# Attention and two feed-forward layers on one core: the probabilities of the later queries turned by DMA

## The chip, the core and the metric

The kernel runs on one core of a Trainium2 chip. TensorE multiplies matrices (PE in the rows, its weight loads PEld), VectorE (DVE) and ScalarE (ACT) work element by element, SyncE (SP) issues all the transfers; GpSimd (POOL) does next to nothing here. Operands lie in SBUF, matmul results in the banks of PSUM. The metric is the device time of one execution in microseconds. The kernel before took 786.69 us (median of 3 runs, 785.3 to 787.19).

## What is computed

Causal attention by blocks of 64 over 4 batches and 8 heads, 576 positions, 64 values a head; then two feed-forward layers on the 2304 tokens. Cut to what matters:

```python
scores = q @ k.T / sqrt(64); scores[block_i < block_j] = -1e9       # blocks of 64
attn = exp(scores - max) / (sum + 1e-9);  x = attn @ v              # (2304, 512)
h = x @ w_in; x2 = (max(h, 0) + log1p(exp(-abs(h)))) @ w_out        # 512 -> 2048 -> 512
h = x2 @ u_in; s = h * softmax(h)                                   # 512 -> 1024
out = ((s - mean) / sqrt(var + 1e-6) * g) @ u_out                   # 1024 -> 512
```

## The kernel before

All large products are made from operands split in two parts of the fast 32-bit matmul format (a high part and the remainder), three matmuls each, so that little precision is lost. Probabilities times v and the transposes run in plain float32.

The work falls into four kinds of tasks. **UnitA** (16 of them, a batch and a pair of heads each) does attention for the queries 0 to 255. **UnitC** (16) does it for the queries 256 to 575, in three tiles of scores `i` = 0, 1, 2: 128 queries of both heads against 384 keys, 128 against 512, and the last 64 queries of both heads, stacked in 128 rows, against 576. **Pair** (72) takes two blocks of 128 of the 2048 hidden columns of the first layer for a chunk of 256 tokens: two blocks of twelve matmuls into `hp`, the softplus, and two blocks of twelve into `acc` (`gh` and `gl` are the parts of its result). **Tok** (18) does the second layer for 128 tokens: 24 matmuls into `h`, the normalisation, and 24 into `op`. **Piece** converts weights. The pairs of the chunks 4 to 8 need what the UnitC tasks deliver, four units to 256 or more tokens; the second layer needs the weights u1 and u2, whose conversion starts when the last unit has left its memory.

Inside a unit C tile `i` goes: scores by `mm_qk` into the two banks of `S`, `mask`, `max`, `scale` (the maximum by 1/8), `exp` into `eC`, `den0`, `den1`, `norm`, then `tr` (lines 470 to 476), which turns every 128 x 128 block of `eC` on TensorE into the bank `T`, and `copy`, which brings `T` into `ps` (the last 64 keys of tile 2 into `p4`). `pv` multiplies `ps` and `p4` by v into `O`, and `x_hi` and `x_lo` split `O` for the pairs. In `eC`, `ps` and `p4` there is one buffer each, so tile `i` of the next unit can't be exponentiated before this unit's has been turned, and no copy into `ps` can start before the PV before it is through.

The order of every engine's instructions is fixed when the program is built. `Plan` simulates the tasks with a duration for each and puts on every engine, whenever it is free, the ready task of the lowest rank. The rank is a task's place plus `RANK` of its group plus `OFF` of its kind; tasks that two engines can do go where they would end sooner. Engines then run their lists strictly in order and wait where an operand is late.

The token stage has the technique that the change brings to the units: `split_hi` and `split_lo` copy the upper and lower 16 bits of `e` apart, `tr` (line 962) turns both halves by a DMA on SP's queue, and `merge` (line 965) puts them together again:

```python
SP.dma_start_transpose(out=self.hlt.bitcast(U16)..., in_=self.hl.bitcast(U16))
DVE.tensor_copy(self.ct.bitcast(U16)..., self.hlt.bitcast(U16)...)   # 2048 16-bit values a row
```

## Time and profile before

| what | value |
|---|---|
| median of 3 runs | 786.69 us |
| profiled execution | 785.26 us, its span 783.5 us |
| TensorE | busy 759.4 us (97%) |
| VectorE | busy 595.2 us (76%) |
| ScalarE | busy 416.6 us (53%) |
| opening, until TensorE is full | 0 to about 60 us |
| units C, first scores to last PV | 188 to 486 us |
| first h, first op | 548.5, 611.2 us |

Busy time counts matmuls and computing instructions; matmuls are pipelined, so their durations overlap. A name such as `eC<-S,mC` is what an instruction writes and reads; a line such as L236 can be that of a helper that many tasks use (228 makes all matmuls, 234 and 236 are copies on ScalarE and VectorE). The clock is the share of full speed that was granted to TensorE.

### The profile page before, as it was taken

Reading aid. Unit: us, or ns where it says so; the run is one execution under the profiler, and the core shown is the slowest. Engines: PE = TensorE matmul, PEld = TensorE weight load, DVE = VectorE, ACT = ScalarE, POOL = GpSimd, SP = SyncE. Lnnn points to the kernel's source line nnn. Section 1 sums busy time; section 2 is a strip of 40 time slices with the busy share of each in tenths; the row PEclk is TensorE's granted clock in tenths of the full one; section 3 lists DMA queues with packets and bytes.
Section 4 is the critical chain, followed back from the end, with each engine's and each line's share of the span. In section 5 each row is a group of like instructions: output and inputs, shape, how many; then the busy total and the mean of one; then the engine's idle time right before and its main releaser. Section 6 shows DMA issues by size and latency. Waiting matters only on the chain.

```text
span 783.5 us, 14248 instructions
## 1 busy us (share of the span) xinstructions
PE 759.4 (97%) x5608; PEld 675.4 (86%) x5608; DVE 595.2 (76%) x1326; ACT 416.6 (53%) x860; POOL 0.7 (0%) x6
## 2 busy tenths in 40 slices
PE   6679999999999999999999999999999999999998
PEld 4469899989888888888888889999998888888887
DVE  6999999475666677667766773766599998799882
ACT  6667765665566556556555554454484433333321
POOL 0000000000000000000000000000000000000000
PEclk9899999999999999999999999999999999999999
DMA  6554552211121112112111200323434453443323
GB/s 215 189 180 162 172 177 66 82 43 43 44 78 59 43 44 69 43 44 70 43 44 43 83 5 29 108 81 103 141 108 95 95 119 88 102 108 88 66 76 82
DMA packets 68643, 69.08 MB, mean 88 GB/s; under 512 B 40288, under 2 KB 51808, under 8 KB 68576
## 3 DMA queue, kind: packets, MB, share of 16 engines
q1 hardware_dynamic: 68576, 68.17, 30.0%
q8 instruction: 44, 0.72, 0.4%
q14 instruction: 23, 0.19, 0.1%
HBM read 49.29 MB, written 9.44 MB: 75 GB/s over the span
## 4 chain that ended last, share of the span: by engine, by line
PE 86%; DVE 10%; issue 1%; DMA 1%; ACT 1%; SPq 0%
PE acc L228 21%; PE hp L228 21%; PE op L228 13%; PE h L228 12%; PE S L228 5%; PE O L228 5%; PE T L476 5%; PE R L228 2%; DVE a L304 2%; DVE w L318 2%; DVE a L308 1%; PE r L228 1%; DVE mA L568 1%; DVE eA L589 1%; DVE t L681 1%
## 5 line engine op out<-in xcount | busy, mean ns | idle before, releaser
L228 PE MATMUL hp<-xt,w 128*128 128x256 f32 x1728 | 218.5, 280 | 2.2 <-DVE t L681 1.4
L228 PEld LDWEIGHTS hp<-xt,w 128*128 128x128 f32 x1728 | 205.4, 188 | 6.0 <-issue 2.7
L228 PE MATMUL acc<-gh,w 128*128 128x256 f32 x768 | 150.2, 285 | 3.5 <-DVE gh L236 3.5
L228 PEld LDWEIGHTS acc<-gh,w 128*128 128x128 f32 x768 | 123.4, 191 | 4.5 <-DVE gh L236 3.9
L228 PE MATMUL acc<-gl,w 128*128 128x256 f32 x384 | 107.6, 280 | 0.9 <-DVE gl L689 0.9
L228 PE MATMUL h<-u,w 128*128 128x512 f32 x432 | 100.4, 389 | 0.0
L228 PE MATMUL op<-w,w2w 128*128 128x512 f32 (+1 forms) x456 | 100.3, 378 | 0.0
L228 PEld LDWEIGHTS op<-w,w2w 128*128 128x128 f32 x456 | 82.5, 188 | 16.0
L228 PEld LDWEIGHTS h<-u,w 128*128 128x128 f32 x432 | 80.9, 188 | 16.6
L456 ACT ACTIVATE eC<-S,mC 128x384 f32<-128x384 f32 (+2 forms) x80 | 51.9, 653 | 52.3 <-DVE mC L445 52.3
L228 PEld LDWEIGHTS acc<-gl,w 128*128 128x128 f32 x384 | 73.1, 190 | 1.1 <-DVE gl L689 1.1
L672 ACT ACTIVATE t<-hp 128x512 f32<-128x512 f32 x72 | 42.7, 593 | 38.0 <-PE hp L228 37.9
L681 DVE SCALAR_TENSOR_TENSOR t<-hp,t 128x512 f32<-128x512 f32 x72 | 48.8, 678 | 17.5 <-ACT t L678 17.2
L689 DVE TENSOR_TENSOR gl<-t,gh 128x512 fp32r<-128x512 f32 x72 | 49.6, 689 | 5.6 <-ACT gh L234 4.5
L228 PE MATMUL acc<-gh,w2w 128*128 128x256 f32 x256 | 49.8, 284 | 0.0
L234 ACT ACTIVATE hl<-e 128x1024 bf16<-128x1024 bf16 x17 | 17.9, 1056 | 59.1 <-DVE e L922 59.1
L678 ACT ACTIVATE t<-t 128x512 f32<-128x512 f32 x72 | 45.5, 631 | 2.0
L675 ACT ACTIVATE t<-t 128x512 f32<-128x512 f32 x72 | 45.6, 633 | 1.8
L441 DVE TENSOR_REDUCE mC<-S 128x2 f32<-128x768 f32 (+2 forms) x48 | 46.3, 964 | 0.1
L234 ACT ACTIVATE ps<-T 128x512 f32<-128x512 f32 (+1 forms) x55 | 30.5, 555 | 29.3 <-PE T L476 29.3
L476 PE MATMUL T<-ident,eC 128*128 128x128 f32 x288 | 46.1, 278 | 0.0
L228 PEld LDWEIGHTS acc<-gh,w2w 128*128 128x128 f32 x256 | 40.8, 189 | 0.2 <-issue 0.2
(159 smaller groups left out, 1136.3 us busy)
## 6 DMA issues: line engine op xcount, KB each, us to landing
raw<-in_w_dram SPq DMA_DIRECT2D x32, 512.0 KB, 3.8
qkC<-in_qk_dram SPq DMA_DIRECT2D x16, 480.0 KB, 3.5
raw_u<-in_u_dram SPq DMA_DIRECT2D x11, 512.0 KB, 3.5
v<-in_vP_dram SPq DMA_DIRECT2D x16, 320.0 KB, 2.9
x2s<-stg SPq DMA_DIRECT2D x18, 256.0 KB, 2.2
xr<-x2s SPq DMA_DIRECT2D x18, 256.0 KB, 3.2
qkA<-in_qkA_dram SPq DMA_DIRECT2D x16, 256.0 KB, 3.5
out_dram<-ob SPq DMA_DIRECT2D x15, 256.0 KB, 2.9
```

The source lines that it names most:

```text
L228: PE.matmul(out, lhsT, rhs, start=start, stop=stop, skip_group_check=True)
L234: ACT.activation(out, a, AF.Copy)
L304: DVE.scalar_tensor_tensor(out=self.a, in0=self.raw[:, :, 1], scalar=-0x80000000, in1=self.a, op0=ALU.bitwise_and, op1=ALU.bitwise_or)
L318: DVE.tensor_sub(self.lo, self.af, self.hi)
L441: DVE.tensor_reduce(out=self.m[:, 0:n], in_=self.scores(i), axis=AX.X if i < 2 else AX.XY, op=ALU.max, negate=True)
L456: ACT.activation(e, sc, AF.Exp, scale=0.125, bias=m[:, j:j + 1], accum_out=den[:, j:j + 1])
L476: PE.transpose(T[:, 128 * k:128 * k + 128], e[:, 128 * k:128 * k + 128], ident)
L672: ACT.activation(self.t, self.hp, AF.Abs)
L675: ACT.activation(self.t, self.t, AF.Exp, scale=-1.0)
L678: ACT.activation(self.t, self.t, AF.Ln, bias=1.0)
L681: DVE.scalar_tensor_tensor(out=self.t, in0=self.hp, scalar=0.0, in1=self.t, op0=ALU.max, op1=ALU.add)
L689: DVE.tensor_sub(self.gl, self.t, self.gh)
```

## The change

The transposes of the units C leave TensorE. `norm` may now run on ScalarE too. Two `split`s per tile copy the lower and the upper 16 bits of the probabilities apart into a new tile `hl`, on ScalarE or VectorE; one DMA turns all blocks of the tile back into `eC`; two `merge`s (one for each head) bring them into `ps`, with `merge4` for `p4`. Tile 2 is padded by 64 columns for this. The bank `T` becomes a third bank of `S`, and the tiles take two of the three in turn. The factor 1/8 moves from `scale` and `exp` to the rounding of the queries, which makes `qk_hi` and `qk_lo` two instructions each. v has one buffer in place of two. The tables `OFF` and `RANK` are new throughout, so the order of everything is. In the token stage either half may be copied by ScalarE, and two dependences were added.

```diff
--- before.py
+++ after.py
-    "Pair.a": -81.8, "Pair.abs": 864.6, "Pair.b": -32.5, "Pair.do_gh": 2361.6, "Pair.do_gl": -1004.4,
+    "Pair.a": 788.0, "Pair.abs": 20664.3, "Pair.b": 1798.0, "Pair.do_gh": 10919.3, "Pair.do_gl": -8219.4,
...
+BANKS = (slice(0, 2), slice(0, 3, 2), slice(1, 3))
...
-            self.t_v = add("SP", dma_ns(327680), -8, self.load_v, [opened, self.t_qk] + g(p2, "t_pv") + g(p1, "t_v"), DMA_LAT)
-            sfree, tfree = (p1.sfree, p1.tfree) if p1 else ([], [])
-            self.t_tr, cps = [[], [], []], []
+            self.t_v = add("SP", dma_ns(327680), -8, self.load_v, [opened, self.t_qk] + g(p1, "t_pv", "t_v"), DMA_LAT)
+            self.t_tr, self.t_mg, self.t_exp, cps = [None, None, None], [[], [], []], {}, []
             for i, w in enumerate(WC):
-                r, heads = 7.0 * i, (0, 1) if i < 2 else (0,)
-                self.t_mm = t = add("PE", (600, 760, 860)[i], r, partial(self.mm_qk, i), [self.t_ql] + sfree)
+                r, heads = 7.0 * i, ((0, 1), (1, 0), (0,))[i]
+                free = [u.t_exp[x] for u, x in ((p1, (1, 0)), (p1, (2, 0))) if u] if i == 0 else \
+                       [self.t_exp[0, 0]] + ([p1.t_exp[2, 0]] if p1 else []) if i == 1 else [self.t_exp[0, 1], self.t_exp[1, 1]]
+                self.t_mm = t = add("PE", (721, 893, 797)[i], r, partial(self.mm_qk, i), [self.t_ql] + free)
                 if i < 2:
                     t = add("DVE", 140, r, partial(self.mask, i), [t])
-                t = chain("DVE", r, ((dve_ns(w * len(heads)), partial(self.max, i)), (140, partial(self.scale, i))), [t])
-                sfree = []
+                t = add("DVE", dve_ns(w * len(heads)), r, partial(self.max, i), [t])
+                e = []
                 for j in heads:
-                    sfree.append(add("ACT", 250 + .833 * w, r, partial(self.exp, i, j), [t] + sfree + (p1.t_tr[i] if p1 else [])))
-                t = chain("DVE", r, ((140, partial(self.den0, i)), (140, partial(self.den1, i))), sfree)
-                for j in heads:
-                    n = add("DVE", 70 + .55 * w, r, partial(self.norm, i, j), [t])
-                    for part in ((0,) if i < 2 else (0, 1)):
-                        m = 3 + i if i < 2 else (4, 1)[part]
-                        x = add("PE", 60 + 110 * m, r + 5, partial(self.tr, i, j, part), [n] + tfree)
-                        self.t_tr[i].append(x)
-                        c = add({"ACT": 110 + 107 * m, "DVE": 90 + 133 * m}, None, r + 4, partial(self.copy, i, j, part), [x] + g(p1, "t_pv"))
-                        tfree = [c]
-                        cps.append(c)
-            self.sfree, self.tfree = sfree, tfree
+                    e.append(add("ACT", 250 + .833 * w, r, partial(self.exp, i, j), [t] + e + (p1.t_mg[i] if p1 else [])))
+                    self.t_exp[i, j] = e[-1]
+                t = chain("DVE", r, ((140, partial(self.den0, i)), (140, partial(self.den1, i))), e)
+                n = [add({"ACT": 100 + .833 * w, "DVE": 70 + .55 * w}, None, r, partial(self.norm, i, j), [t]) for j in heads]
+                cols, back = w * len(heads), [p1.t_tr[i]] if p1 else []
+                n = [add({"ACT": 100 + .833 * cols, "DVE": 75 + .52 * cols}, None, r, partial(self.split, i, k), n + back) for k in range(2)]
+                self.t_tr[i] = add("SP", 300 + 1.6 * cols, r, partial(self.tr, i), n, 2600.0)
+                for j in range(2):
+                    self.t_mg[i].append(add("DVE", 75 + .52 * cols, r + 4, partial(self.merge, i, j), [self.t_tr[i]] + g(p1, "t_pv")))
+                if i == 2:
+                    self.t_mg[i].append(add("DVE", 205, r + 4, self.merge4, [self.t_tr[i]] + g(p1, "t_pv")))
+                cps += self.t_mg[i]
...
-            copy(e, self.qk[0], self.qr)
+            q, k = slice(0, 384), slice(384, 960)
+            if e == "ACT":
+                ACT.activation(self.qk[0][:, q], self.qr[:, q], AF.Copy, scale=0.125)
+                ACT.activation(self.qk[0][:, k], self.qr[:, k], AF.Copy)
+            else:
+                DVE.tensor_scalar(self.qk[0][:, q], self.qr[:, q], 0.125, None, op0=ALU.mult)
+                DVE.tensor_copy(self.qk[0][:, k], self.qr[:, k])
 
         def qk_lo(self):
-            DVE.tensor_sub(self.qk[1], self.qr, self.qk[0])
+            q, k = slice(0, 384), slice(384, 960)
+            DVE.scalar_tensor_tensor(out=self.qk[1][:, q], in0=self.qr[:, q], scalar=0.125, in1=self.qk[0][:, q],
+                                     op0=ALU.mult, op1=ALU.subtract)
+            DVE.tensor_sub(self.qk[1][:, k], self.qr[:, k], self.qk[0][:, k])
...
-            self.v = self.t([128, 2, 5, D], "v")
+            self.v = self.t([128, 2, 5, D], "v", 1)
...
-            return state["S"][:, :, 0:WC[i] if i < 2 else WC[2] // 2]
+            return state["S"][:, BANKS[i], 0:WC[i] if i < 2 else WC[2] // 2]
...
-        def scale(self, i):
-            DVE.tensor_scalar(self.m[:, 0:self.n], self.m[:, 0:self.n], 0.125, None, op0=ALU.mult)
...
-            ACT.activation(e, sc, AF.Exp, scale=0.125, bias=m[:, j:j + 1], accum_out=den[:, j:j + 1])
+                e = e[:, 0:WC[2]].rearrange("p (a b) -> p a b", a=2)
+            ACT.activation(e, sc, AF.Exp, bias=m[:, j:j + 1], accum_out=den[:, j:j + 1])
...
-        def norm(self, i, j):
-            e = state["eC"][i][:, j, :]
-            DVE.tensor_scalar(e, e, self.stat[i][1][:, j:j + 1], None, op0=ALU.mult)
-
-        def tr(self, i, j, part):
-            T, e = state["T"], state["eC"][i][:, j, :]
-            if part:
-                PE.transpose(T[0:64, 0:128], e[:, 512:576], ident)
-                return
-            for k in range(3 + i if i < 2 else 4):
-                PE.transpose(T[:, 128 * k:128 * k + 128], e[:, 128 * k:128 * k + 128], ident)
-
-        def copy(self, i, j, part, e):
-            T, ps, p4 = state["T"], state["ps"], state["p4"]
-            if part:
-                copy(e, p4, T[0:64, 0:128])
-            elif i < 2:
-                copy(e, ps[:, 0:3 + i, j, 128 * i:128 * i + 128], T[:, 0:384 + 128 * i].rearrange("p (t q) -> p t q", q=128))
+        def norm(self, i, j, e):
+            p, r = state["eC"][i][:, j, 0:WC[i]], self.stat[i][1][:, j:j + 1]
+            if e == "ACT":
+                ACT.activation(p, p, AF.Copy, scale=r)
             else:
-                copy(e, ps[:, :, :, 256:320], T.rearrange("p (t j q) -> p t j q", t=4, j=2))
+                DVE.tensor_scalar(p, p, r, None, op0=ALU.mult)
+
+        def split(self, i, n, e):
+            p = state["eC"][i].rearrange("p j w -> p (j w)").bitcast(U16).rearrange("p (c two) -> p c two", two=2)
+            to = state["hl"][i].bitcast(U16).rearrange("p (two c) -> p two c", two=2)
+            cols = WC[i] * (2 if i < 2 else 1)
+            copy(e, to[:, n, 0:cols], p[:, 0:cols, n])
+
+        def turned(self, i):
+            return state["eC"][i].rearrange("p j w -> p (j w)").bitcast(U16)
+
+        def tr(self, i):
+            SP.dma_start_transpose(out=self.turned(i).rearrange("p (c q) -> p c q", q=128), in_=state["hl"][i].bitcast(U16))
+
+        def merge(self, i, j):
+            ps = state["ps"].bitcast(U16)
+            if i < 2:
+                src = self.turned(i).rearrange("p (two j t q) -> p j t q two", two=2, j=2, q=128)[:, j]
+                dst = ps[:, 0:3 + i, j, 256 * i:256 * i + 256]
+            else:
+                src = self.turned(i).rearrange("p (two t j q) -> p j t q two", two=2, j=2, q=64)[:, j, 0:4]
+                dst = ps[:, :, j, 512:640]
+            DVE.tensor_copy(dst.rearrange("p t (q two) -> p t q two", two=2), src)
+
+        def merge4(self):
+            src = self.turned(2).rearrange("p (two t q) -> p t q two", two=2, q=128)[0:64, 4]
+            DVE.tensor_copy(state["p4"].bitcast(U16).rearrange("p (q two) -> p q two", two=2), src)
...
-        state["S"] = q.tile([128, 2, 512], F32, name="S")
-        state["T"] = q.tile([128, 512], F32, name="T")
+        state["S"] = q.tile([128, 3, 512], F32, name="S")
         state["O"] = q.tile([128, 512], F32, name="O")
-        state["eC"] = [state["pat"].tile([128, 2 if i < 2 else 1, w], F32, name=f"eC{i}") for i, w in enumerate(WC)]
+        state["eC"] = [state["pat"].tile([128, 2 if i < 2 else 1, w], F32, name=f"eC{i}") for i, w in enumerate((WC[0], WC[1], WC[2] + 64))]
+        state["hl"] = [state["pat"].tile([128, (2 * w if i < 2 else w + 64)], F32, name=f"hl{i}") for i, w in enumerate(WC)]
+        DVE.memset(state["hl"][2], 0.0)
...
-            self.t_sp = [add({"ACT": 950, "DVE": 610}, None, rank, self.split_hi, [t_c, t_w] + o2("t_tr")),
-                         add("DVE", 610, rank, self.split_lo, [t_c, t_w] + o2("t_tr"))]
+            self.t_sp = [add({"ACT": 950, "DVE": 610}, None, rank, partial(self.split, i), [t_c, t_w] + o2("t_tr")) for i in range(2)]
             t_s = chain("DVE", rank, [(75, partial(self.small1, i)) for i in range(4)], [t_c])
             t_s = add("ACT", 335, rank, self.logexp, [t_s])
             self.t_s = chain("DVE", rank, [(75, partial(self.small2, i)) for i in range(3)], [t_s] + o3("t_ob"))
             self.t_tr = add("SP", 3000, rank + .5, self.tr, self.t_sp + o2("t_mg"), DMA_LAT)
             self.t_mg = add("DVE", 1140, rank, self.merge, [self.t_tr] + o2("t_ll"))
-            self.t_lh = add({"ACT": 950, "DVE": 610}, None, rank, self.ln_hi, [self.t_mg] + o2("t_b"))
-            self.t_ll = add("DVE", 1140, rank, self.ln_lo, [self.t_lh])
+            self.t_lh = add({"ACT": 950, "DVE": 610}, None, rank, self.ln_hi, [self.t_mg, pairs[-1].t_b1] + o2("t_b"))
+            self.t_ll = add("DVE", 1140, rank, self.ln_lo, [self.t_lh, pairs[-1].t_b1] + o2("t_b"))
...
-        def split_hi(self, e):
-            self.hl, self.hlt, self.ct = (state[x][self.t % 2] for x in ("hl", "hlt", "ct"))
-            kind = BF16 if e == "ACT" else U16
-            copy(e, self.hl.bitcast(kind)[:, DF2:], self.half(1, kind))
-
-        def split_lo(self):
-            self.hl, self.hlt, self.ct = (state[x][self.t % 2] for x in ("hl", "hlt", "ct"))
-            DVE.tensor_copy(self.hl.bitcast(U16)[:, 0:DF2], self.half(0, U16))
+        def split(self, i, e):
+            self.hl, self.hlt, self.ct = (state[x][self.t % 2] for x in ("hl2", "hlt", "ct"))
+            halves = self.e.bitcast(U16).rearrange("p (f two) -> p f two", two=2)
+            copy(e, self.hl.bitcast(U16)[:, DF2 * i:DF2 * i + DF2], halves[:, :, i])
```

Where an order stands below, a row is line, operation, what it writes and reads, the shape and a count. On TensorE in the units, where `T` is the bank of the transposes, `S` that of the scores, and `hp` and `acc` belong to pairs; before:

```order
L228 MATMUL hp_114<-xt,w_8_89 128x256 x12
L476 MATMUL T<-ident,eC_2173 128x128 x4
L228 MATMUL hp_114<-xt,w_9_90 128x256 x12
L228 MATMUL S<-qkh 128x512 x2
L228 MATMUL S<-qkl,qkh 128x512 x2
L228 MATMUL S<-qkh,qkl 128x512 x2
L473 MATMUL T<-ident,eC_2173 64x128
L228 MATMUL acc<-gh,w_4_101 128x256
```

and now:

```order
L230 MATMUL hp_114<-xt,w_8_89 128x256 x12
L230 MATMUL hp_114<-xt,w_9_90 128x256 x12
L230 MATMUL S<-qkh 128x512 x2
L230 MATMUL S<-qkl,qkh 128x512 x2
L230 MATMUL S<-qkh,qkl 128x512 x2
L230 MATMUL acc<-gh,w_4_101 128x256
```

The groups into `T` are gone from between the pair blocks and the scores; the rest of the piece stands as it did.

On VectorE from the maximum of a tile 2 to that of a later tile (`qkl` is the low part of the next unit's q and k, `t` and `gl` are a pair's); before:

```order
L441 TENSOR_REDUCE mC<-S 128x1
L413 TENSOR_TENSOR qkl<-qkC,qkh 128x960
L445 TENSOR_SCALAR mC<-mC 128x1
L236 COPY ps<-T 128x4x128
L460 TENSOR_SCALAR dC<-dC 128x1
L464 RECIPROCAL dC<-dC 128x1
L468 TENSOR_SCALAR eC_2173<-eC_2173,dC 128x576
L436 MEMSET S 64x2x64
L681 SCALAR_TENSOR_TENSOR t<-hp_115,t 128x512
L441 TENSOR_REDUCE mC<-S 128x2
```

and now:

```order
L453 TENSOR_REDUCE mC<-S 128x1
L238 COPY hl_2158<-eC_2155 128x1024
L423 SCALAR_TENSOR_TENSOR qkl<-qkC,qkh 128x384
L425 TENSOR_TENSOR qkl<-qkC,qkh 128x576
L501 COPY ps<-eC_2154 128x3x256 x2
L468 TENSOR_SCALAR dC<-dC 128x1
L709 TENSOR_TENSOR gl<-t,gh 128x512
L472 RECIPROCAL dC<-dC 128x1
L479 TENSOR_SCALAR eC_2156<-eC_2156,dC 128x576
L448 MEMSET S 64x2x64
L238 COPY hl_2159<-eC_2156 128x576
L453 TENSOR_REDUCE mC<-S 128x2
```

The scaling of the maximum and the copy out of `T` have gone; splits (`hl<-eC`) and merges (`ps<-eC`) of other tiles have come between, and a pair's `gl` now stands behind the merges of the next unit's tile 0.

## Rows read from the trace of the kernel before

**Rows 1.** Page, busy tenths of 40 equal slices of the span, by engine.

```profile
PE   6679999999999999999999999999999999999998
...
DVE  6999999475666677667766773766599998799882
```

**Rows 2.** Windows from PV to PV: length, busy us (instructions) by engine, clock, DMA.

```profile
317.62:336.00 18.38, 18.38 (x156) 16.25 (x157) 12.73 (x34) 10.46 (x21) 0.00 (x0) 1.00 0.17 47
336.00:354.27 18.27, 18.27 (x156) 16.14 (x157) 12.72 (x34) 10.45 (x21) 0.00 (x0) 1.00 0.16 46
...
sum 201.61, PE 201.61 PEld 178.16 DVE 140.27 ACT 116.89 POOL 0.00; mean PE 18.33 PEld 16.20 DVE 12.75 ACT 10.63 POOL 0.00
```

**Rows 3.** Chain that ended last, shares of the span by engine, tile, line.

```profile
by line: PE acc L228 21.5%; PE hp L228 21.3%; PE op L228 12.5%; PE h L228 12.5%; PE S L228 4.9%; PE O L228 4.8%; PE T L476 4.6%; PE R L228 1.9%; DVE a L304 1.8%; DVE w L318 1.5%; DVE a L308 1.4%; issue 1.3%; PE r L228 1.2%; DVE mA L568 1.1%
```

**Rows 4.** Timeline of TensorE, one unit: start us, us, instruction, count.

```profile
322.23 0.43 PE L228 MATMUL S<-qkh,qkl 128*128 128x288 f32 x2
...
331.52 0.60 PE L476 MATMUL T<-ident,eC 128*128 128x128 f32 x4
331.87 1.62 PE L228 MATMUL hp<-xt,w 128*128 128x256 f32 x12
```

**Rows 5.** The same chain in order of time, after the units: start, us, what.

```profile
509.23 2.72 PE acc L228 x24
```

**Rows 6.** Groups by line and shape, VectorE: count, busy us, mean ns, idle before.

```profile
L965 DVE COPY ct<-hlt 128x2048 uint16<-128x2048 uint16 x18 | 21.9, 1218 | 5.4 <-DMA hlt<-hl 5.4
...
L468 DVE TENSOR_SCALAR eC<-eC,dC 128x512 f32<-128x512 f32 x32 | 14.4, 480 | 0.2
...
L959 DVE COPY hl<-e 128x1024 uint16<-128x1024 uint16 x18 | 12.4, 692 | 0.4
...
L236 DVE COPY ps<-T 128x512 f32<-128x512 f32 x14 | 9.7, 692 | 10.1 <-PE T L476 10.1
...
L236 DVE COPY ps<-T 128x384 f32<-128x384 f32 x11 | 6.1, 552 | 0.2 <-PE T L476 0.2
...
L445 DVE TENSOR_SCALAR mC<-mC 128x2 f32<-128x2 f32 x32 | 5.1, 161 | 0.6
...
L236 DVE COPY p<-T 64x128 f32<-64x128 f32 x15 | 4.2, 283 | 0.0
...
L236 DVE CAST xt<-O 128x192 fp32r<-128x192 f32 x8 | 2.8, 354 | 6.6 <-PE O L228 6.6
```

**Rows 7.** The same groups, ScalarE.

```profile
L234 ACT ACTIVATE ps<-T 128x512 f32<-128x512 f32 x34 | 20.3, 597 | 19.6 <-PE T L476 19.6
...
L234 ACT ACTIVATE hl<-e 128x1024 bf16<-128x1024 bf16 x17 | 17.9, 1056 | 59.1 <-DVE e L922 59.1
...
L234 ACT ACTIVATE ps<-T 128x384 f32<-128x384 f32 x21 | 10.3, 488 | 9.8 <-PE T L476 9.8
```

**Rows 8.** DMA issues: count, KB each, median us from issue to landing.

```profile
qkC<-in_qk_dram SPq DMA_DIRECT2D x16, 480.0 KB, 3.5
v<-in_vP_dram SPq DMA_DIRECT2D x16, 320.0 KB, 2.9
...
hlt<-hl SPq DMA_TRANSPOSE x18, 4.3
```

**Rows 9.** Timeline of VectorE, the same unit: the normalisation of the last scores.

```profile
327.28 0.52 DVE L468 TENSOR_SCALAR eC<-eC,dC 128x576 f32<-128x576 f32 x1
```

**Rows 10.** Windows of 20 us, opening.

```profile
20.00:40.00 20.00, 12.00 (x84) 8.45 (x82) 19.08 (x52) 13.46 (x36) 0.00 (x0) 0.83 0.62 198
```

**Rows 11.** Timelines of VectorE and TensorE around the first h.

```profile
537.62 0.69 DVE L318 TENSOR_TENSOR u<-a_u,u 128x512 fp32r<-128x512 f32 x1
...
548.51 11.06 PE L228 MATMUL h<-u,w 128*128 128x512 f32 x48
```

**Rows 12.** Timeline of all engines at the end.

```profile
747.05 33.11 PE L228 MATMUL op<-w,w2w 128*128 128x512 f32 x168
...
771.87 1.23 DVE L975 TENSOR_TENSOR w2w<-ct,w2w 128x1024 fp32r<-128x1024 f32 x1
```

More of the change, by code (lines that the diff above doesn't have):

```diff
@@ L30 @@
-    "Piece.do_lo@P": 1123.5, "Piece.do_lo@P0": -1265.3, "Piece.do_lo_g": -389.9, "Piece.load": 727.8,
-    "Piece.load@P0": -81.6, "Tok.a": 281.7, "Tok.aggr": -1508.4, "Tok.bm": 1627.8, "Tok.center": -2327.7,
-    "Tok.exp": 1006.4, "Tok.ln_hi": 147.1, "Tok.ln_lo": 1789.8, "Tok.load": -1361.3, "Tok.logexp": -1108.4,
-    "Tok.max": -2583.3, "Tok.merge": 1445.4, "Tok.mul": 348.2, "Tok.o_evac": -1055.5, "Tok.small1": -386.7,
-    "Tok.small2": -428.2, "Tok.split_hi": 1311.4, "Tok.split_lo": -1105.9, "Tok.stats": 584.7, "Tok.store": -419.8,
@@ new lines @@
+    "Pair.evac": 675.0, "Pair.exp": -7474.3, "Pair.ln": -9835.0, "Pair.store": -5836.4, "Pair.stt": 7547.0,
+    "Piece.abs": 10964.5, "Piece.abs@P0": 2481.0, "Piece.bits0": 2651.5, "Piece.bits0@P0": -10740.6,
+    "Piece.bits1": -5638.9, "Piece.bits1@P0": 1504.7, "Piece.bits2": -6724.4, "Piece.bits2@P0": 8160.9,
+    "Piece.do_hi": 6783.4, "Piece.do_hi@P0": 8530.5, "Piece.do_hi_g": 2688.1, "Piece.do_lo": 4827.0,
+    "Piece.do_lo@P": -4177.2, "Piece.do_lo@P0": -15153.1, "Piece.do_lo_g": -860.1, "Piece.load": 10384.6,
@@ new lines @@
+    "Piece.load@P0": 11156.8, "Tok.a": -3408.6, "Tok.aggr": -9655.0, "Tok.bm": 2985.1, "Tok.center": -10058.0,
+    "Tok.exp": 13414.8, "Tok.ln_hi": 6845.7, "Tok.ln_lo": 3377.4, "Tok.load": -6979.6, "Tok.logexp": -4391.2,
+    "Tok.max": 7574.5, "Tok.merge": -6856.4, "Tok.mul": -2725.4, "Tok.o_evac": 6544.2, "Tok.small1": 5810.6,
+    "Tok.small2": -1482.8, "Tok.split": -6804.0, "Tok.split_hi": -9056.3, "Tok.split_lo": -9326.4,
+    "Tok.stats": -5464.0, "Tok.store": 22167.6, "Tok.tr": -13756.9, "Tok.x_hi": -11484.4, "Tok.x_lo": -1305.6,
[11 rows of a table added]
@@ L50 @@
+    "UnitC.copy": -4765.8, "UnitC.den0": 5224.6, "UnitC.den1": -6300.5, "UnitC.exp": -5258.0, "UnitC.load_qk": 3996.6,
+    "UnitC.load_v": -4166.3, "UnitC.mask": -654.7, "UnitC.max": -9211.3, "UnitC.merge": 1083.9,
+    "UnitC.merge4": 3115.7, "UnitC.mm_qk": -3221.1, "UnitC.norm": 5503.0, "UnitC.pv": -8282.1, "UnitC.qk_hi": 34.6,
+    "UnitC.qk_lo": -14155.2, "UnitC.split": -696.2, "UnitC.tr": -11789.9, "UnitC.x_hi": 13549.6,
+    "UnitC.x_lo": -4037.3, "UnitC.xx": 5329.0,
 }
 RANK = {
[3 rows of a table removed]
-    "Tok": (798.2, 267.06),
[3 rows of a table added]
@@ L56 @@
+    "Tok": (18449.2, 1582.9),
 }
@@ L429, in mm_qk @@
                         h = slice(64 * j, 64 * j + 64)
-                        mm(S[:, j, 0:w], q[h, 128 * i:128 * i + 128], k[h, 384:384 + w], n == 0, n == 2)
+                        mm(S[:, j], q[h, 128 * i:128 * i + 128], k[h, 384:384 + w], n == 0, n == 2)
                     else:
-                        mm(S[:, j, 0:w // 2], q[:, 256:384], k[:, 384 + w // 2 * j:384 + w // 2 * (j + 1)], n == 0, n == 2)
+                        mm(S[:, j], q[:, 256:384], k[:, 384 + w // 2 * j:384 + w // 2 * (j + 1)], n == 0, n == 2)
         def mask(self, i):
-            DVE.memset(state["S"][0:64, :, WC[i] - 64:WC[i]], MASKED)
+            DVE.memset(self.scores(i)[0:64, :, WC[i] - 64:WC[i]], MASKED / 8)
         def max(self, i):
@@ L441, in max @@
             DVE.tensor_reduce(out=self.m[:, 0:n], in_=self.scores(i), axis=AX.X if i < 2 else AX.XY, op=ALU.max, negate=True)
-            self.n = n
-        def scale(self, i):
-            DVE.tensor_scalar(self.m[:, 0:self.n], self.m[:, 0:self.n], 0.125, None, op0=ALU.mult)
             self.stat = getattr(self, "stat", {})
-            self.stat[i] = (self.m, self.den, self.n)
+            self.stat[i] = (self.m, self.den, n)
         def exp(self, i, j):
@@ L763, in open_3 @@
         p3 = left.enter_context(pool("p3", "left"))
-        for x in ("hl", "hlt", "ct"):
+        for x in ("hl2", "hlt", "ct"):
             state[x] = [p3.tile([128, DF2], F32, name=f"{x}{i}") for i in range(2)]
```

14 lines of the change are left out of this document (1 added, 13 removed), and 28 rows, old and new, of tables (OFF, RANK).

## The prediction

> **What bounds the kernel now.** I read the slices of the page first. TensorE's line is at nine tenths from the fourth slice to the end; only the opening (slices of 19.6 us at 6, 6 and 7 tenths) has gaps, together about 21 us, and there VectorE's line rises to nine [rows 1]. So from about 60 us on the end is set by how much TensorE has to do. Next the windows cut at the PV matmuls of the attention units (the 16 units of queries from 256 on): eleven periods are 18.33 us each on average, TensorE is busy for all of it, VectorE for 12.75 us, ScalarE for 10.63 [rows 2]. In this stage a microsecond taken from TensorE shortens the run, as long as the others can follow. The chain of waits agrees: it is on TensorE nearly throughout and gives the transposes into T 4.6% [rows 3]. The profiled execution took 785.26 us, 1.76 us more than its span of 783.5, and lies 1.4 us under the median of 786.69; my sum starts from 785.26.
>
> **TensorE.** Removed are 19 transposes in each unit, 304 in all; scores and PV matmuls stay as they are. What one is worth has three readings. From start to start a group of four holds the engine for 0.35 us [rows 4], 0.09 each, 27 us for 304: the lower end, since it counts nothing that is lost ahead of a group's first start. By the chain, 4.6% of 783.5 is 36.0 us, 2.25 in a unit [rows 3]. By difference: 24 pair matmuls in a row take 2.72 us [rows 5], so a unit's 96 take 10.9; with some 2.4 for scores (the chain's 4.9% for S over 16 units) and 2.35 for PV (its 4.8%), 18.33 leaves 2.7 us, or 43 us for 16 units [rows 2, 3]. I take the chain's 36.0, the middle one: it counts what the end was delayed by. TensorE then needs 18.33 - 2.25 = 16.1 us a unit.
>
> **VectorE.** The 16-bit copies are not new to this kernel: the token stage does the same even-and-odd copies. 1024 values take 0.692 us and 2048 take 1.218, so 0.167 us plus 0.513 ns a value [rows 6]. The new order puts 50 of the 96 splits on VectorE: 19 of 768 values (0.561), 15 of 1024 (0.692), 16 of 576 (0.463), 28.4 us. The merges are all on VectorE: 32 of 768, 32 of 1024, 32 of 512 (0.430) and 16 of 256 (0.298), 58.5 us. The subtraction for qkl becomes two instructions, 16 x 0.167 = 2.7, and six more 512-wide casts come over, 2.9. Gone are 48 scalings (0.161, 7.7 us), the copies out of T (9.7 + 6.1 + 4.2 = 20.0 us), 37 normalisations that go to ScalarE (at 0.480, 17.8) and 20 casts of the output (at 0.354, 7.1) [rows 6]. Net +40 us, 2.5 a unit: 12.75 + 2.5 = 15.3 of 16.1 us, 95%. Starts follow each other a little closer than these durations say, so 92% may be nearer. VectorE is not the bound by this sum, but it has hardly a microsecond left in a unit, which is the weak spot of the forecast.
>
> **ScalarE.** 1024 values take 1.056 us there and 512 take 0.597, so about 0.14 us plus 0.9 ns a value [rows 7]. It takes 46 splits (13 of 768, 17 of 1024, 16 of 576: 39 us), 37 normalisations (about 0.55: 20) and 20 output casts (about 0.3: 6), and loses the copies out of T (20.3 + 10.3) and six casts (3.6) [rows 7]: +31 us, 1.9 a unit, 12.6 of 16.1 us. Covered.
>
> **The transposes by DMA.** 48 are added, of 1536, 2048 and 1280 16-bit columns. The token stage has the widest one already: it lands 4.3 us after its issue [rows 8]. I take 4.3 for all three; the smaller ones can be quicker. They go through SP's queue between the loads of v and qk. v has one buffer now, so its load waits for the PV before; in the order it stands ahead of the second transpose, which is not ready until the scores that precede that PV have been turned into probabilities, so nothing ready stands behind it.
>
> On this the Trainium skill speaks against the change: "VectorE: DVE Perf Modes", section "The three transpose paths", gives 390 ns for a 128x128 block on TensorE and 1309 ns by DMA, and its rules say to use TensorE where PSUM will do. A unit moves 12 + 16 + 10 = 38 such 16-bit blocks; at that price an estimate is 49.7 us a unit, far beyond 16.1, and the sum would be a loss of hundreds of microseconds. The trace does not bear it out: sixteen blocks land together in 4.3 us.
>
> **Does the chain within a unit still fit?** Before, the last scores of a unit end at 322.66 and their normalised row is done at 327.80, 5.1 us later [rows 4, 9]. From there the new path is split 0.65, landing 4.3, merges 2 x 0.43 + 0.30, with hops between engines about 0.5: 6.6 us, 11.7 in all. On TensorE the new order leaves 11.2 to 15.1 us of other work between those scores and PV (seven to nine pair blocks of some 1.4 us and the next unit's scores); in six units it is 11.4. VectorE's own work in the same stretch, summed along the order, is 6.8 to 14.0 us and leaves 1.0 to 4.6. So some units may wait a few tenths, 0 to 6 us in all; I take 2.
>
> **Opening and token stage.** The order of the opening is nearly the old one; six casts of weights leave VectorE and a copy of 768 comes, under 2 us either way: 0. After the last PV the u1 pieces are converted one at a time, and their last subtraction starts at 537.62 while the first h starts at 548.51 [rows 11]: 10.2 us to spare. The order leaves 36 pair matmuls less in between, 4.1 us: still covered. At the end 120 output matmuls of full width stood between the last h and the last output block, 27 us; now 96, 21.8. The chain they cover ran from 747 to 773.1, 26 us, but with VectorE and ScalarE busy with the token before; its own steps come to some 17. Taken at 0; at worst 4 us [rows 12]. Sum: 785.26 - 36.0 + 2 = **751.3 us**.
>
> **Rivals.** *VectorE sets the pace of the units.* At 95% of the period, with every instruction in a fixed order, a late landing or a late exponential stops everything queued behind it, the pairs' subtractions too, and TensorE then waits for those. For it: VectorE waited 5.6 us of each 18.33 before, and 0.8 would be left. Against: much of that was waiting for TensorE, which itself comes sooner. One microsecond a unit gives 751.3 - 2 + 16 = 765; from 756 to 780. Such gaps should not cost the clock: its mean of 0.83, a mixture of the levels 1.2 and 2.4 GHz, stands where TensorE was busy 12 of 20 us [rows 10], and here it would be busy 16 of 17.
>
> *Slower: the 16-bit copies cost more than in the token stage.* Here the merges write runs of 256 values into strided rows of ps and the splits read two heads. If each such value cost 1.9 times the row's, the 5.4 us a unit would be 10.3 and VectorE 20.2 us a unit, against 18.33 now: 785 + 16 x 1.9 = 815. It decides from 1.6 times on, where VectorE reaches 18.33. Against: they pick every other 16-bit value just as L959 and L965 do, on one side of the copy.
>
> *Slower: the transposes go one behind the other, with the loads.* If no transpose overlapped another transfer, a unit would need 3 x 4.3 us, 3.5 for qk and 2.9 for v [rows 8], 19.3 us against 18.33: 785 + 16 = 801. It decides from 18.33 on. Against: in the token stage the landing stays at 4.3 although loads run beside it in the same queue. The block price of the Trainium skill ("VectorE: DVE Perf Modes", "The three transpose paths") would be the extreme of this rival and shares its chance.
>
> *The gain does not come.* The longer path through the DMA holds a unit at 18.3 us although TensorE has less to do; 785.
>
> *Better.* The new order also closes part of the opening's 21 us; 735 to 742.
>
> **How the numbers follow.** Forecast 0.66 (742 to 756: the three readings of the transposes and 0 to 6 us of waits); VectorE sets the pace 0.22; copies dearer 0.04; transposes in a row 0.03; no gain 0.02; better 0.03. The range 742 to 768 holds the forecast and about two thirds of the first rival, 0.8. About 0.3% is what a measurement of this kernel can tell from no change, 2.4 us. Faster 0.66 + 0.22 + 0.03 = 0.91, same 0.02, slower 0.07.
>
> **What would show it.** Right: periods between PVs near 16.1 us times the pair blocks in them, TensorE busy throughout, VectorE above 90% there; the transposes landing in 3 to 4.5 us; merges of 1024 near 0.69. Wrong: idle time of TensorE ahead of PV or of acc matmuls, released by the merges or by gl; VectorE at ten tenths over the units; landings over 6 us.

## The result, and the profile after

The changed kernel took 762.22 us (median, 761.21 to 762.49) where the kernel before took 786.94 beside it: 0.9686 of the time, 95% interval 0.9669 to 0.9704, 24.7 us less. The forecast was 751.3, 35.4 below the median of 786.69 known then. The time lies in the range of 742 to 768, above the 742 to 756 of the forecast's own case.

The profiled execution took 761.21 us, its span is 759.3 (before 783.5): 24.2 less. Its page, busy time and then the slices that answer [rows 1]:

```profile
PE 729.9 (96%) x5304; PEld 645.3 (85%) x5304; DVE 638.4 (84%) x1376; ACT 441.0 (58%) x907; POOL 0.7 (0%) x6
...
PE   6779999999999999999999999999999999999998
...
DVE  6999999576888998888898995767999988888882
```

TensorE's line is as full as it was, and VectorE's has risen to eight and nine tenths from the eleventh slice to the twenty-fourth, where the attention units lie. The windows that answer [rows 2], first from the first PV to the last, then the one unit with a full set of scores and eight blocks of pair matmuls, as nearly all periods of the kernel before have (length, busy us and count by engine, clock, DMA share, GB/s):

```profile
211.59:464.83 253.24, 251.22 (x2053) 219.76 (x2053) 225.28 (x500) 185.35 (x378) 0.00 (x0) 1.00 0.61 129
...
434.18:450.60 16.42, 16.42 (x136) 14.28 (x135) 15.97 (x36) 13.68 (x28) 0.00 (x0) 1.00 0.48 97
```

A unit of eight blocks takes 16.42 us where it took 18.33, and VectorE works in 89% of the stage (225.28 of 253.24). What TensorE waited for between 200 and 470 us (total, times, longest), three of the chain's longest pieces, and the merges by shape (count, busy us, mean ns, idle before), which answer [rows 3, 6]:

```profile
PE S L230 <- ACT eC L464: 3.5, 3, 1.5
```

```profile
198.53 6.82 DMA eC<-hl
...
354.83 6.91 DMA eC<-hl
403.04 6.50 DMA eC<-hl
```

```profile
L501 DVE COPY ps<-eC 128x768 uint16<-128x768 uint16 x32 | 29.5, 945 | 0.1
L501 DVE COPY ps<-eC 128x1024 uint16<-128x1024 uint16 x32 | 21.2, 683 | 5.2 <-DMA eC<-hl 5.1
L501 DVE COPY ps<-eC 128x512 uint16<-128x512 uint16 x32 | 12.7, 417 | 2.7 <-DMA eC<-hl 2.7
```

So three waits were left, each begun by a transpose that landed after 6.5 to 6.9 us. The third, along the engines (SP: the load of v and the transpose behind it; VectorE; ScalarE; TensorE):

```profile
402.42 0.33 SPq L429 DMA_DIRECT2D v<-in_vP_dram  x1
403.04 3.03 SPq L491 DMA_TRANSPOSE eC<-hl  x1
```

```profile
409.57 0.69 DVE L501 COPY ps<-eC 128x1024 uint16<-128x1024 uint16 x1 [1.62 <-DMA eC<-hl]
...
410.96 0.94 DVE L453 TENSOR_REDUCE mC<-S 128x2 f32<-128x768 f32 x1
```

```profile
411.93 0.58 ACT L464 ACTIVATE eC<-S,mC 128x384 f32<-128x384 f32 x1 [0.83 <-DVE mC L453]
```

```profile
413.74 0.50 PE L230 MATMUL S<-qkh 64*128 64x512 f32 x2 [1.12 <-ACT eC L464]
```

The merge stands on VectorE ahead of the maximum of the next unit's scores. It comes 1.62 us late, so the maximum, the exponential and the release of the score banks come late, and TensorE stands for 1.12 us.

**Where the 24.2 us came from.** The kernel after has other amounts of pair work in each stage, so the stages are compared with every pair matmul at 0.113 us [rows 5].

| mark in the profiled execution, us | before | after | e9 (below) |
|---|---|---|---|
| first scores | 182.72 | 183.33 | 185.35 |
| first PV | 207.61 | 211.59 | 208.21 |
| last PV | 483.47 | 464.83 | 456.24 |
| first h | 548.51 | 525.78 | 523.71 |
| span | 783.5 | 759.3 | 758.7 |

Transposes gone, 304 at 0.097 us (experiment e9): -29.6. Waits in the units: +3.5. The first scores come 0.6 us later although 12 pair matmuls (1.4 us) less stand ahead of them: +2.0. Together -24.1. After the last PV nothing is lost: the order has 48 pair matmuls less there, 5.4 us, and that stretch is 5.6 us shorter.

### The profile page after: what moved, and what is told of

Its sections match the earlier page's. It is cut to its first block, busy times and chain, and to the rows that moved or that the text cites. A ratio compares the mean times of both kernels' runs of the same rounds, so it can differ in the third digit from the quotient of the medians.

```text
span 759.3 us, 13917 instructions
## 1 busy us (share of the span) xinstructions
PE 729.9 (96%) x5304; PEld 645.3 (85%) x5304; DVE 638.4 (84%) x1376; ACT 441.0 (58%) x907; POOL 0.7 (0%) x6
## 4 chain that ended last, share of the span: by engine, by line
PE 76%; DVE 16%; DMA 4%; ACT 2%; issue 2%; SPq 0%; ACTq 0%; DVEq 0%
PE acc L230 19%; PE hp L230 19%; PE op L230 13%; PE h L230 13%; PE O L230 4%; PE S L230 4%; DMA eC<-hl 3%; PE R L230 2%; DVE ps L501 2%; DVE a L306 1%; DVE w L320 1%; DVE mA L588 1%; DVE a L310 1%; DVE t L701 1%; PE r L230 1%
## 5 line engine op out<-in xcount | busy, mean ns | idle before, releaser
L230 PE MATMUL acc<-gh,w 128*128 128x256 f32 x768 | 146.4, 283 | 3.5 <-DVE gh L238 3.5
L501 DVE COPY ps<-eC 128x768 uint16<-128x768 uint16 (+2 forms) x96 | 63.4, 681 | 7.9 <-DMA eC<-hl 7.8
L230 PE MATMUL acc<-gh,w2w 128*128 128x256 f32 x256 | 48.0, 280 | 0.0
L236 ACT ACTIVATE hl<-eC 128x1024 uint16<-128x1024 uint16 (+2 forms) x46 | 39.2, 861 | 8.5 <-DVE eC L479 8.0
L999 ACT ACTIVATE ob<-op,A 128x512 f32<-128x512 f32 (+1 forms) x19 | 12.7, 667 | 50.6 <-PE op L230 50.5
```

What stands on the lines that cost most here:

```text
L230: PE.matmul(out, lhsT, rhs, start=start, stop=stop, skip_group_check=True)
L236: ACT.activation(out, a, AF.Copy)
L501: DVE.tensor_copy(dst.rearrange("p t (q two) -> p t q two", two=2), src)
L999: ACT.activation(self.ob[:, cols], self.o[cols.start][:, cols], AF.Copy, scale=self.A)
```

## Experiments

**What the transposes were worth.** The forecast took 36.0 us, and the account above leaves 29.6. My theory was that their worth was 0.098 us each; three kernels made from the kernel before measure it, one with every group made twice, one with none, one with a single transpose a group.

e1:

```diff
-                PE.transpose(T[0:64, 0:128], e[:, 512:576], ident)
+                for _ in range(2):
+                    PE.transpose(T[0:64, 0:128], e[:, 512:576], ident)
...
-            for k in range(3 + i if i < 2 else 4):
+            for k in 2 * list(range(3 + i if i < 2 else 4)):
```

> The kernel before, with every group of transposes into T made twice in a row (304 more transposes, the result is the same). It measures what one transpose is worth to TensorE. Theory, from the two traces: between the first and the last PV the changed kernel took 22.6 us less, with 36 more pair matmuls (4.1 us), 6 fewer score matmuls (0.8 us) and 2.0 us of waiting, so 285 transposes were worth about 27.9 us, 0.098 us each; 304 more should cost 30 us, about 817. Rival, the prediction's term by the chain of waits: 36.0 us, 0.118 each, about 823. If the removed time were the busy time of the groups (0.16 each), 51 us, 838.

Measured: 823.11 us (821.96 to 823.87), 1.0466 of before (1.0447 to 1.0484), 36.7 more. That is the rival's number and the forecast's, and for doubling my theory was wrong. A doubled group in its timeline:

```profile
328.76 1.03 PE L477 MATMUL T<-ident,eC 128*128 128x128 f32 x8
329.55 1.66 PE L228 MATMUL hp<-xt,w 128*128 128x256 f32 x12
```

Eight transposes hold the engine from start to start for 0.79 us where four held it for 0.35 [rows 4]: the second four cost 0.44. Doubling is not the reverse of removing, so the two had to be tried the other way:

e9:

```diff
         def tr(self, i, j, part):
+            return
...
         state["T"] = q.tile([128, 512], F32, name="T")
+        DVE.memset(state["T"], 0.0)
```

> The kernel before with all 304 transposes of the probabilities left out (the bank T is filled once with zeros and the copies out of it stay, so the attention of the later queries is not computed). Nothing else of the change is in it, so it measures what their removal can give by itself. Theory: a group of transposes replaces a change-over between two other groups that comes back when it goes; the periods of the kernel after with eight pair blocks (16.42 us against 18.325) give 1.9 us a unit, 30.5 in all: 786.3 - 30.5 = 756. Rival: they are worth what the chain of waits says and what doubling them cost, 36 to 36.7: 750. If 756, five and a half of the missing microseconds were never there to gain; if 750, the changed kernel loses them elsewhere.

e10:

```diff
-            for k in range(3 + i if i < 2 else 4):
+            for k in range(1):
...
+        DVE.memset(state["T"], 0.0)
```

> The kernel before with one transpose left in each of the six groups of a unit (96 of 304; the rest of T keeps zeros, so the attention of the later queries is not computed). Theory: each transpose beyond a group's first costs the 0.120 us that it cost when doubled, so 208 fewer give 25.0: 761.3, and the first of a group costs only some 0.057, so that the step from here to none at all is 5.5. Rival: every transpose costs the same 0.118: 761.8, and the step to none is 11.4. A third reading, 0.100 each throughout: 765.5.

Measured: none 760.05 us (759.57 to 760.5), 0.9663 of before (0.965 to 0.9676), 26.3 less; one a group 766.78 (766.09 to 768.1), 0.9751 (0.9735 to 0.9766), 19.6 less. The same thirteen periods between PVs in the four kernels, in the order before, none, twice, one a group:

```profile
225.99:464.14 238.15, 238.15 (x1990) 210.44 (x1990) 165.01 (x414) 138.14 (x282) 0.00 (x0) 1.00 0.17 51
```

```profile
224.70:438.79 214.09, 214.09 (x1743) 186.24 (x1743) 163.56 (x414) 134.45 (x282) 0.00 (x0) 1.00 0.19 56
```

```profile
230.75:498.64 267.89, 267.89 (x2238) 239.88 (x2237) 165.51 (x414) 138.46 (x282) 0.00 (x0) 1.00 0.15 45
```

```profile
223.61:445.05 221.44, 221.44 (x1822) 193.54 (x1821) 166.02 (x414) 135.81 (x282) 0.00 (x0) 1.00 0.18 54
```

Both expectations of e9 were too low, and that of e10 nearest to the measurement is the third reading, 0.100 each. TensorE is busy throughout in all four stretches. 13 x 19 = 247 transposes less shorten the stretch by 24.06 us, 0.097 each; 247 more lengthen it by 29.74, 0.120 each; the 169 that e10 takes out are worth 16.71, 0.099 each. That the first of a group costs only 0.057 falls with e10 (the theory said 761.3), since the step from one a group to none is 7.4 us for 78, 0.094 each. Removing 304 measures 29.6 us in the units, and doubling measures more than removing; most of that difference is not the transposes', as shown below.

At the end only 26.3 arrive (24.8 in the profiled execution). The marks say where the rest went: the first scores come 2.6 us later (more on that at the end of the experiments), and from the last PV to the first h, where e9 runs what before runs, it takes 67.47 us and before 65.04. Two stretches of 10 us there, before and e9, and 24 matmuls of e9 in its chain, beside those in [rows 5]:

```profile
500.00:510.00 10.00, 10.00 (x91) 10.00 (x90) 6.88 (x12) 4.50 (x9) 0.00 (x0) 1.00 0.46 160
```

```profile
480.00:490.00 10.00, 10.00 (x87) 10.00 (x86) 7.05 (x13) 4.25 (x7) 0.00 (x0) 1.00 0.29 99
```

```profile
488.54 2.83 PE acc L228 x24
```

The same matmuls at the same granted clock of 1.00, the 2.4 GHz level, take 2.83 us a block of 24 instead of 2.72, and keep that pace for all 22 blocks of the stretch: 22 x 0.11 = 2.4 us. The changed kernel has 2.72 there, and both paces in its units. What sets the pace I can't say.

The pace is in the doubling too. A group of transposes and the block behind it in the chain, before and in e1:

```profile
236.68 0.59 PE T L476 x4
237.27 1.38 PE acc L228 x12
```

```profile
242.64 1.02 PE T L477 x8
243.66 1.42 PE acc L228 x12
```

Read from the starts of all matmuls in the four stretches above, a pair matmul mostly follows the pair matmul ahead of it after about 113 ns or about 118 ns. It is 118 for 352 of 1170 before, for 554 of 1196 with no transposes, for 972 of 1170 with twice as many and for 730 of 1170 with one a group; against before this costs 1.0, 2.8 and 1.7 us. At the pace of before, removing would be worth 25.1 us in the stretch (0.102 a transpose, 30.9 for 304), doubling 27.0 (0.109), and the 169 of e10 18.4 (0.109), which leaves 6.7 for the last 78 (0.086). So doubling and removing differ much less than they seem to, and the first transpose of a group does cost less than the others, though not as little as 0.057. Whether the edits set the pace is not known.

**Is VectorE the bound now?** e3 makes every merge into `ps` twice, e2 makes the two of tile 0 in one instruction with the heads outermost.

```diff
-            DVE.tensor_copy(dst.rearrange("p t (q two) -> p t q two", two=2), src)
+            for _ in range(2):
+                DVE.tensor_copy(dst.rearrange("p t (q two) -> p t q two", two=2), src)
```

> The changed kernel with every merge made twice in a row (the result is the same): 112 more copies, 68 us more of VectorE at the durations of the changed kernel's trace, 4.2 us a unit. VectorE was busy for 199.2 of 223.4 us between the PVs of 227 and 450 us, so it has some 24 us free there. Theory, VectorE is near the limit but not at it: the free time takes up part, and the run is 35 to 55 us longer, with TensorE waiting throughout the units (800 to 815). If VectorE had been the limit already, all 68 us would show (830). If there was still room, under 20 us.

Measured: 817.83 us, 55.6 more than the changed kernel and a little above the 800 to 815 expected. It is a single execution, so its spread is not known, and the granted clock of the stretch was 0.98 where the changed kernel had 1.00. From the first PV to the last, and what TensorE waited for in the units:

```profile
216.62:519.07 302.45, 266.68 (x2053) 226.49 (x2052) 283.10 (x584) 185.31 (x378) 0.00 (x0) 0.98 0.51 108
```

```profile
PE S L230 <- ACT eC L464: 26.0, 21, 2.6
PE O L230 <- DVE ps L502: 7.3, 7, 1.9
PE S L230 <- DVE qkl L425: 4.8, 7, 1.7
```

VectorE is busy 65.0 us more (703.4 to 638.4), and the run is 55.6 longer: there is hardly room for more work on it. The other way:

```diff
+            if i == 0:
+                if j == 0:
+                    src = self.turned(i).rearrange("p (two j t q) -> p j t q two", two=2, j=2, q=128)
+                    dst = ps[:, 0:3, :, 0:256].rearrange("p t j (q two) -> p j t q two", two=2)
+                    DVE.tensor_copy(dst, src)
+                return
```

> The changed kernel, but the two merges of tile 0 (768 values each, 0.945 us each in the changed kernel where the rows of other widths gave 0.561) are one instruction over both heads, with the heads as the outermost dimension (1536 values); the order of everything is otherwise the same. If the odd number of three rows is what slows them, the one instruction takes about 0.167 + 1536 x 0.000513 = 0.96 us in place of 1.89, 15 us less of VectorE in all. Theory: TensorE waits only at three places, for late landings, so the time falls by 1 us at most (761 to 762). Rival, VectorE sets the pace of the units: nearly a microsecond a unit comes back, and the time falls by 5 us or more.

Measured: 760.13 us (759.73 to 762.12), 0.9676 (0.9657 to 0.9695); the interval overlaps that of the changed kernel.

```profile
L499 DVE COPY ps<-eC 128x1536 uint16<-128x1536 uint16 x16 | 15.3, 956 | 1.4 <-PE O L230 0.9 <-DMA eC<-hl 0.5
```

1536 values in one instruction take hardly longer than 768 did. 14.2 us leave VectorE's merges, the waits in the units fall from 3.5 to 1.6 us, and the median by 2.1, which is not clear of the noise. So VectorE does not set the pace, but with e3 beside it it stands near the edge from which on it does.

**The late landings.** Are the loads of q, k and v to blame? e6 leaves 30 of the 32 out (all units compute with the first one's operands), e7 has GpSimd issue them, e11 is e2 with a load put behind the next transpose on SP's queue where that was planned shortly after, e12 is e11 with the tables of before.

> The changed kernel without the loads of qk and v for all units of the later queries but the first: those units compute with the first one's data. 30 of 32 loads are left out, the order is otherwise the same. Theory: the three waits of TensorE in the units (1.52, 0.90 and 1.12 us) come from transposes that were issued within a microsecond behind a load and landed 6.5 to 6.9 us later instead of 3.9; without loads all land in about 4, and the time falls by some 3.5 us, to about 758.7. Rival: the landings are late because transposes of 2048 columns follow each other, or VectorE is the limit: long landings stay, and the time stays at 762.

Measured: 760.56 us (759.18 to 761.0), 0.9669 (0.9652 to 0.9686). The transposes land in 3.3, 3.7 and 5.7 us (least, median, most) instead of 3.4, 3.9 and 6.9, and the waits in the units are 0.6 us. The theory's size for them is borne out, its time of 758.7 is not: the first scores stand at 186.58 us in this profile, 3 us later than in the changed kernel's, with a clock of 0.74 between 20 and 40 us where the changed kernel has 0.83.

```diff
-            SP.dma_start(out=self.qr, in_=qk[self.b, self.pr])
+            POOL.dma_start(out=self.qr, in_=qk[self.b, self.pr])
...
-            SP.dma_start(out=self.v, in_=vP[self.b, :, 2 * self.pr:2 * self.pr + 2])
+            POOL.dma_start(out=self.v, in_=vP[self.b, :, 2 * self.pr:2 * self.pr + 2])
```

> The changed kernel with the loads of qk and v of the later queries' units issued by GpSimd in place of SyncE, at the same places of the order. Theory: a transpose then need not stand behind a load in the same queue; if the queue is what delays it, landings are near 4 us and the time falls by about 3 us, to 759. Rival: the transfer engines are shared whichever queue issues, the landings beside a load stay at 6 us or more, and the time stays at 762 or rises, if GpSimd's issues come later than SyncE's.

Measured: 770.0 us (769.45 to 772.41), 0.9797 (0.9778 to 0.9817), 7.8 more than the changed kernel. The transposes' landings, and TensorE's waits in the units:

```profile
DMA to landing us min/median/max: 3.4/4.4/9.1
```

```profile
PE S L230 <- ACT eC L464: 7.2, 6, 1.9
PE O L230 <- DVE ps L501: 1.8, 3, 1.2
```

Another queue makes the landings later still, so the transposes are not late because they stand in one queue behind a load; it seems to go with another transfer being under way.

```diff
...
+            if u is not None and u.key == "UnitC.tr" and u.at - t.at < (1500.0 if t.key == "UnitC.load_qk" else 3000.0):
+                order.remove(t)
+                order.insert(order.index(u) + 1, t)
```

> The changed kernel with the joint merge of tile 0, and with the loads of qk and v put behind the next transpose on SP's queue where a transpose was planned up to 1.5 us (qk) or 3 us (v) after them. Theory: the late landings behind loads and the slow merge make the 3.5 us of waits in the units: landings no later than 5.5 us, under 1 us of waits, 762.2 - 3 = 759. Rival: the waits come from the order being as tight as it is, whichever transfer is late; the loads then come late in their turn, and the time stays at the 760.1 of the joint merge alone or above.

Measured: 759.88 us (759.27 to 760.82), 0.966 (0.9646 to 0.9675): the fastest of all, level with e2 and with e9. But its landings are no better:

```profile
DMA to landing us min/median/max: 3.4/4.3/7.0
```

```profile
PE S L236 <- ACT eC L470: 2.0, 2, 1.1
```

Its longest landing, 7.0 us from 198.38, has a load 2.2 us behind it and none shortly ahead. So a load behind a transpose seems to delay it as one ahead does, and the theory of the order on the queue falls, as the rival had it. In e6 that same transpose still needed 5.7 us with no load under way, so loads are not its whole story. Another candidate is the next transpose. In the changed kernel all four landings over 6.0 us (6.48 to 6.91) had a load under way and also the next transpose issued 3.5 to 5.2 us behind them, before they were done; with a load and no other transpose the longest was 6.0, and in e6 the two longest, 5.7 and 5.4, had the next one 2.8 and 3.0 us behind. How much belongs to each was not separated, and a late landing is by itself likelier to be overtaken by the next issue.

> The same with the kernel before's tables of ranks. With those tables alone the changed kernel took 761.48, with waits of 1.4 us in the units. Theory: as above, 761.5 - 1.5 to 2 = 759.5 to 760. Rival: no difference, 761.5.

Measured: 761.27 us (759.81 to 762.32), 0.9677 (0.966 to 0.9694): no difference from e4, as the rival had it.

**The order made anew.** e4 is the changed code with the old `OFF` and `RANK`, e5 the old code with the new ones, e8 the changed kernel with its opening ordered by the old tables.

> The changed kernel planned with the tables of offsets and ranks of the kernel before; everything else of the change is kept. It tells what the new order is worth. Theory: the transposes off TensorE bring about 30 us with any order that keeps TensorE supplied, but the old ranks were not made for the longer way through the DMA, so TensorE waits some microseconds more in the units: 765 to 775. Rival: the gain is mostly the order's, and the time is near the kernel before, 780 or more.

> The kernel before, planned with the new tables of offsets and ranks alone. Theory: TensorE is full from 60 us on whatever the order, so the time moves little, 785 to 792, the upper end if the new order of the opening loses some 2 us here too. Rival: the new order alone brings some of the gain, 780 or less.

> The changed kernel with the opening (attention of the first 256 queries, the conversion of w1 and w2 and the first 16 pairs) planned with the old tables, ahead of the rest; on VectorE and TensorE the first 340 and 460 rows stand exactly as in the kernel before. The rest is planned with the new tables and comes out nearly but not exactly as in the changed kernel. Theory: the changed kernel lost 2.0 us in the opening, where TensorE and VectorE waited for a load of weights at 79 to 84 us; here the units start 2 us earlier, and the time is about 760 unless the units lose it again. Rival: the 2 us do not matter, since the opening is made up for later: 762.

Measured: e4 761.48 us (759.48 to 761.88), 0.968 (0.9663 to 0.9698); e5 793.89 (793.24 to 795.03), 1.0102 (1.0087 to 1.0118); e8 763.71 (761.99 to 765.77), 0.9718 (0.9695 to 0.9741). The new tables bring nothing to the new code and cost the old code 7.8 us, more than the theory's 785 to 792; both theories of e4 asked too much. In the order of e5 the old code does not compute the right result (perhaps for want of the two dependences that the change adds), so its time says only what that order costs, and 2 us of it are the pace: 955 pair matmuls of its units follow at 118 ns, 447 before. e8 does not bring the 2 us of the opening back, but it doesn't settle them either: its first scores stand at 185.48 us with a clock of 0.74 between 20 and 40 us, and its units take longer too. The 2 us may be no property of the change at all: in e9, where the order of the opening is that of before, the first scores came 2.6 us later than in the profile of before. Its clock was 0.74 between 20 and 40 us, with TensorE busy 13.4 of the 20, where [rows 10] have 0.83, both mixtures of the levels 1.2 and 2.4 GHz:

```profile
20.00:40.00 20.00, 13.39 (x84) 9.71 (x84) 17.92 (x48) 12.71 (x33) 0.00 (x0) 0.74 0.57 188
```

## Why the prediction was right, and where it was off

**The bound and the sign: right.** What leaves TensorE shortens the run while the others follow. e9 shows the removal alone at 760.05; the changed kernel with its DMA path is 2.2 us above that, and with the joint merge (e2, e11) level with it. That is in part chance, as e9's profile has 2.6 us of a later opening and 2.4 us of the slow pace behind the units.

**The worth of the transposes: the step that failed.** Of 27, 36.0 and 43 I took "the chain's 36.0, the middle one". Removing them is worth 29.6 us in the units and 26.3 at the end, so the reading from start to start, 27 us and called the lower end, was the nearest one; even at one pace throughout it is 30.9 and not 36.0. The chain gives the group at 236.68 us 0.59, while its four transposes hold the engine from start to start for 0.41. The reason given against the lower reading was that it counts nothing lost ahead of a group's first start. That loss exists, but it is one of a hand-over between two groups and for the most part does not leave with the group: another hand-over takes its place. Over the thirteen periods the transposes hold the engine from start to start for 22.4 us (0.091 each), and the gaps between pair matmuls that keep neither pace cost 7.0 us over it before and 4.4 in e9: 22.4 and 2.6, less the 1.0 of pace, make the 24.06. After the scores, without any transpose between, the kernel after still has it:

```profile
447.34 0.39 PE L230 MATMUL S<-qkh,qkl 64*128 64x512 f32 x2
447.66 0.39 PE L230 MATMUL acc<-gh,w 128*128 128x256 f32 x1
447.88 0.28 PE L230 MATMUL acc<-gl,w 128*128 128x256 f32 x1
448.00 0.40 PE L230 MATMUL acc<-gh,w 128*128 128x256 f32 x2
```

The first `acc` matmul is followed after 0.22 us, the next after 0.12. The reading by difference (43) failed the same way: it took every pair block at 2.72 us for 24 and put all their hand-overs down to the transposes. With the account of the marks in place of 36.0 and 2, which is bookkeeping after the fact, the sum is 785.3 - 29.6 + 3.5 + 2.0 = 761.2, against 761.21 in the profiled execution; the 26.3 of e9 would give 761.0 too, but by other losses than those of the changed kernel.

**VectorE and ScalarE: right in the sum, wrong in its terms.** Forecast were 15.3 and 12.6 us a unit; measured over 15 periods, 225.28 / 15 = 15.0 and 185.35 / 15 = 12.4. The merges of 1024 and 512 values came at 683 and 417 ns (0.692 and 0.430 forecast), those of 768 at 945 against 561, 12.3 us more in all. Yet VectorE's busy time rose by 43.2 us (638.4 from 595.2) where 40 were forecast, so the other terms came out some 9 us lower; that the sum held is luck, and they were not taken apart. The merges of 768 have three blocks a head where the others have four; with six blocks in one instruction (e2) the price per value is the old one again. The Trainium skill ("VectorE: DVE Perf Modes", "Mode 2×_2P — use both read ports for one tensor") wants the outermost dimension even, or odd and equal on both sides, for two values a cycle. The rows agree if the source's three blocks, which lie side by side, count as one run of 384 and the destination's as three; that was not tried by itself.

**The transposes by DMA: right in the middle, wrong at the edge.** The median landing is 3.9 us (4.3 taken). The 6.5 to 6.9 of a few was not foreseen; "in the token stage the landing stays at 4.3 although loads run beside it" was a median too, and the prediction itself had named landings over 6 us as a sign against it. They make the waits: 2 us taken out of 0 to 6, 3.5 measured.

**Opening and token stage.** 0 was taken for both. The token stage lost nothing; the opening's 2.0 is at the bound given and within what executions differ.

**The rivals.** 762 lies in the zone of "VectorE sets the pace", but its mechanism is worth 3.5 us in waits, not 16; e3 shows how near it is. That the range of 742 to 768 holds 762.22 is therefore partly luck: its upper part stood there for this rival, and it was the oversized worth of the transposes that needed it. Copies dearer: true of one shape, 1.7 times, too little to decide. Transposes in a row with the loads: no as a price (16.4 us a unit and not 19.3), though the landings up to 3 us over the median stand where a load and a further transpose are under way. No gain: no.

## What to carry to other kernels

An operation taken off the bounding engine was worth little more here than its slot from start to start, since most of the hand-overs that the chain of waits adds to it come back between its neighbours. To measure what a removal is worth, remove it alone, and before two such times are compared look whether the neighbours kept their pace: doubling (36.7 us) seemed to confirm the chain's 36.0 against removing (26.3), and most of the difference was the pace of other matmuls and a later opening. Where a slower engine rises to 89% of a stage, look at the latest landing of what it waits for, not at the median. Before the price of a copy is carried over from one place to another, look whether its number of outer rows is the same kind.

## What was not expected of the hardware

- TensorE keeps one of two paces over a long stretch of the same matmuls at the same granted clock: 2.72 or 2.83 us for 24 of 128x256, 91 or 87 matmuls in 10 us. The share of the slow one differs from kernel to kernel by up to 4 us over a run. The cause is open.
- Twice 768 16-bit values in three rows take 2 x 945 ns on VectorE, 1536 in six rows 956 ns.
- Transposes by DMA that land in 3.9 us in the median need up to 6.9 us beside loads of 320 to 480 KB and a further transpose (7.0 with some loads issued behind them, 9.1 with the loads on GpSimd's queue), 5.7 without the loads.
